# Reading expert weights from the slot that holds them, by register-addressed weight loads, instead of copying them between slots

## The chip, the cores and the metric

One core of one Trainium2 chip. The time is the device time of one execution of the whole kernel, in microseconds (us). Medians are given with the number of runs. A ratio is the mean time of one kernel's fast runs over the mean time of the other's fast runs of the same rounds on the same chip, so it isn't quite the ratio of the medians that stand beside it.

The medians are over all executions; the ratios leave the slow ones out. The kernel before was run again in each group of runs; its medians there were 215.28, 216.62, 215.74 and 217.13 us. The last of these groups (the run with one register-addressed block, and shared_late) was on another chip than the other experiments.

## The reference

Eight sequences of 576 tokens. Each goes through linear attention (8 heads of 64), then as a whole through one of eight experts, chosen by the mean of its tokens:

```python
# attention (Shen): softmax of q over the head dim, of k over the tokens
kv  = einsum('bhsd,bhse->bhde', k_s, v)
x   = einsum('bhsd,bhde->bhse', q_s, kv)        # -> x[8, 576, 512]
# sentence-level mixture of experts
logits = x.mean(axis=1) @ w_gate                # [8, 8]
e_idx  = argmax(logits, axis=1)                 # one expert per sequence
h   = maximum(x[b] @ w1[e], 0)                  # w1[e]: 512 x 1024
out = gate[b] * (h @ w2[e])                     # w2[e]: 1024 x 512
```

The inputs are one fixed draw, in which the experts come out as 2, 3, 3, 1, 3, 3, 4, 6. The kernel may not rely on that: it finds the expert of each sequence while it runs.

## The kernel before

TensorE computes in fp16, but for the gates' small matmuls (64 of the 1703 in the profile, f32). The weights of an expert lie in one of five slots of a ring in SBUF; sequence b has slot b mod 5. If an expert is already in the ring (a small history, searched on VectorE, says in which slot), its load from memory is skipped by a condition, and VectorE copies it from the source slot `src` into the sequence's own slot. If it was loaded fresh, `src` is the slot itself, and the same copies copy it onto itself. So there are always four copies per sequence, two of w1 and two of w2:

```python
    def fetch(b, w_all, part):
        if "src" not in seqs[b]:
            seqs[b]["src"] = nc.values_load(seqs[b]["sidx"][0:1, 0:1], engines=[ET.DVE], ...)
        ...
        copy = nc.vector.tensor_copy(
            out=w_all[:, b % NS, cs, fs],
            in_=w_all[:, ds(seqs[b]["src"], 1), cs, fs].rearrange("p o c f -> p (o c) f"),
        )

    def moe(b):
        xt = seqs[b]["xt"]
        w1_sb, w2_sb = w1_all[:, b % NS], w2_all[:, b % NS]      # constant addresses
        ...
        for fc in range(NF):                    # 8 column blocks of the first layer
            for c in range(ND):                 # 4 wide matmuls, 512 tokens
                nc.tensor.matmul(phm, lhsT=w1_sb[:, c, fsl], rhs=xt[:, c, 0:SM], ...)
            for c in range(ND):                 # 4 narrow ones, the other 64 tokens
                nc.tensor.matmul(pht[...], lhsT=w1_sb[:, c, fsl], rhs=xt[:, c, SM:S], ...)
            ...
            yield                               # attention of later sequences is woven in here
```

One `matmul` becomes two instructions on TensorE, a weight load and a matmul (the profile counts 1703 of each). The first layer of a sequence is 8 blocks of 8 such pairs.

The softmax here doesn't subtract the row's maximum and nothing guards it: scores larger than these inputs give would overflow.

Of the kernel before, what the change touches and what calls it, by code (L numbers as in the profile page):

```python
# [9 lines left out]
FP32 = mybir.dt.float32  # L10
# [3 lines left out]
ALU = mybir.AluOpType  # L14
AX = mybir.AxisListType
ET = mybir.EngineType
# [3 lines left out]
def kernel(  # L20
# [15 lines left out]
    nc = tc.nc  # L36

    B, H, S, Dh = q.shape
    D, E = moe_w_gate.shape
    F = moe_w1.shape[2]  # L40
    J = S // 64
    SM = 512
# [35 lines left out]
    ones_row = consts.tile([1, 128], FP16)  # L78
    nc.vector.memset(ones_row, 1.0)
    hist = consts.tile([1, 8], FP32)  # L80
    nc.vector.memset(hist, -1.0)
    held = consts.tile([1, 8], FP16)
    own = consts.tile([1, NS, 8], FP32)
    nc.vector.memset(own, 0.0)
# [23 lines left out]

    out_p = out.rearrange("b (p j) d -> b p j d", j=J)

    ins, halves, seqs, issued, copies = {}, {}, {}, {}, {}

    def load(n, names="qkv"):
        if n >= 2 * B:
# [146 lines left out]
    def gate_step(b):  # L261
        pooled = seqs[b]["pooled"] if b else seqs["pooled"]
        pg = bank("x") if b else seqs["qb"][0][:, 32:64]
        for c in range(ND):
            nc.tensor.matmul(
                pg[0:1, 0:E], lhsT=pooled[:, c:c + 1], rhs=wg_sb[:, c, :],
                start=(c == 0), stop=(c == ND - 1),
            )
        zz = gat_pool.tile([1, E], FP32, name="zz")
        nc.vector.tensor_single_scalar(out=zz, in_=pg[0:1, 0:E], scalar=1.0 / S, op=ALU.mult)  # L270
        mx8 = gat_pool.tile([1, 8], FP32, name="mx8")
        nc.vector.max(out=mx8, in_=zz)
        eidx = gat_pool.tile([1, 8], U32, name="eidx")
        nc.vector.max_index(out=eidx, in_max=mx8, in_values=zz)
        slot = b % NS
        sidx = None
        if b:
            same = gat_pool.tile([1, 8], FP32, name="same")
            nc.vector.tensor_tensor(
                out=same, in0=hist, in1=eidx[0:1, 0:1].to_broadcast([1, 8]), op=ALU.is_equal  # L280
            )
            score = gat_pool.tile([1, 8], FP32, name="score")
            nc.vector.scalar_tensor_tensor(
                out=score, in0=same, scalar=2.0, in1=own[:, slot], op0=ALU.mult, op1=ALU.max
            )
            top = gat_pool.tile([1, 8], FP32, name="top")
            nc.vector.max(out=top, in_=score)
            fresh = gat_pool.tile([1, 1], U32, name="fresh")
            nc.vector.tensor_single_scalar(out=fresh, in_=top[:, 0:1], scalar=1.0, op=ALU.is_equal)
            sidx = gat_pool.tile([1, 8], U32, name="sidx")  # L290
            nc.vector.max_index(out=sidx, in_max=top, in_values=score)
        nc.vector.tensor_copy(out=hist[:, slot:slot + 1], in_=eidx[0:1, 0:1])

        gone = (b + 2) % NS
        nc.vector.memset(hist[:, gone:gone + 1], -1.0)
        nmx = gat_pool.tile([1, 1], FP32, name="nmx")
        nc.vector.tensor_single_scalar(out=nmx, in_=mx8[:, 0:1], scalar=-1.0, op=ALU.mult)
        e_val = nc.values_load(
            eidx[0:1, 0:1], engines=[ET.Pool], min_val=0, max_val=E - 1,
            skip_runtime_bounds_check_because=IN_RANGE,  # L300
        )
        kw = {}
        if b:
            f_val = nc.values_load(
                fresh, engines=[ET.Pool], min_val=0, max_val=1,
                skip_runtime_bounds_check_because="is_equal gives 0 or 1",
            )
            kw = dict(cond=(f_val == 1))
        w1_src = moe_w1[ds(e_val, 1)].rearrange("o (h c e) f -> h e (o c) f", h=2, c=ND)
        nh = 1 if b else 2  # L310
        issued[b] = []
        for fh in range(nh):
            fs = slice(fh * F // nh, (fh + 1) * F // nh)
            for h in range(2):
                issued[b].append(nc.gpsimd.dma_start(  # L315
                    out=w1_all[64 * h:64 * h + 64, slot, :, fs], in_=w1_src[h][:, :, fs], **kw
                ))
        seqs[b].update(zz=zz, nmx=nmx, sidx=sidx, e_val=e_val, kw=kw)
        if b:
            load_w2(b)  # L320
        for load_inst in issued[b]:
            for copy in copies.get(b - 1, ()):
                apart(load_inst, copy)

    def apart(first, second):
        tc.declare_no_dep(
            first.ins, second.ins,
            reason="the slot that b + 1 loads into is taken out of the history before b looks for its source",
        )
# [41 lines left out]
        nc.vector.tensor_tensor(out=gate, in0=gate, in1=pb[:, 0:1], op=ALU.add)  # L371
        seqs[b]["gate"] = gate

    def fetch(b, w_all, part):

        if "src" not in seqs[b]:
            seqs[b]["src"] = nc.values_load(
                seqs[b]["sidx"][0:1, 0:1], engines=[ET.DVE], min_val=0, max_val=NS - 1,
                skip_runtime_bounds_check_because=IN_RANGE,
            )  # L380
        if w_all is w1_all:
            cs, fs = slice(0, ND), slice(part * (F // 2), (part + 1) * (F // 2))
        else:
            cs, fs = slice(part * (NF // 2), (part + 1) * (NF // 2)), slice(0, D)
        copy = nc.vector.tensor_copy(  # L385
            out=w_all[:, b % NS, cs, fs],
            in_=w_all[:, ds(seqs[b]["src"], 1), cs, fs].rearrange("p o c f -> p (o c) f"),
        )
        copies.setdefault(b, []).append(copy)
        for load_inst in issued.get(b + 1, ()):  # L390
            apart(copy, load_inst)

    def moe(b):
        xt = seqs[b]["xt"]
        w1_sb, w2_sb = w1_all[:, b % NS], w2_all[:, b % NS]
        hsb = h_pool.tile([128, NF, S], FP16, name="hsb")
        pht = bank("ht")
        for fc in range(NF):
            phm = bank("mm")
            fsl = slice(fc * 128, (fc + 1) * 128)  # L400
            for c in range(ND):
                nc.tensor.matmul(  # L402
                    phm, lhsT=w1_sb[:, c, fsl], rhs=xt[:, c, 0:SM],
                    start=(c == 0), stop=(c == ND - 1),
                )
            for c in range(ND):
                nc.tensor.matmul(  # L407
                    pht[:, fc * ST:(fc + 1) * ST], lhsT=w1_sb[:, c, fsl], rhs=xt[:, c, SM:S],
                    start=(fc == 0 and c == 0), stop=(fc == NF - 1 and c == ND - 1),
                )  # L410
            nc.scalar.activation(out=hsb[:, fc, 0:SM], in_=phm, func=AF.Relu)  # L411
            if fc == NF - 1:
                nc.scalar.activation(
                    out=hsb[:, :, SM:S], in_=pht.rearrange("p (c s) -> p c s", c=NF), func=AF.Relu
                )
            yield
        gate = seqs[b]["gate"]
        for st in range(4):
            po = bank("mm")
            for fc in range(NF):  # L420
                nc.tensor.matmul(  # L421
                    po, lhsT=hsb[:, fc, st * 128:st * 128 + 128], rhs=w2_sb[:, fc, :],
                    start=(fc == 0), stop=(fc == NF - 1),
                )
                if fc == 3:
                    yield
            osb = o_pool.tile([128, D], FP32, name="osb")
            nc.scalar.mul(osb, po, gate)  # L428
            for jj in range(2):
                nc.sync.dma_start(out=out_p[b, :, 2 * st + jj], in_=osb[64 * jj:64 * jj + 64])  # L430
            yield
        po = bank("mm")
        HD = D // 2
        for fc in range(NF):
            for dh in range(2):
                nc.tensor.matmul(  # L436
                    po[64 * dh:64 * dh + 64, 0:HD], lhsT=hsb[:, fc, SM:S],
                    rhs=w2_sb[:, fc, dh * HD:(dh + 1) * HD], start=(fc == 0), stop=(fc == NF - 1),
                )
        osb = o_pool.tile([128, HD], FP32, name="osb_t")  # L440
        nc.scalar.mul(osb, po[:, 0:HD], gate)
        for dh in range(2):
            nc.sync.dma_start(
                out=out_p[b, :, J - 1, dh * HD:(dh + 1) * HD], in_=osb[64 * dh:64 * dh + 64]
            )
        yield
# [8 lines left out]
    def at(t, fn, *args):  # L455
        ticks.setdefault(t, []).append((fn, args))
# [10 lines left out]
    at_gate(2, 1)  # L467
    at(9.5, load, 5)
    at(9.6, load, 6)
    places = [(15, 25), (30, 35), (41, 46), (58, 64), (74, 80), (91, 97)]  # L470
    for b in range(2, B):
        for i in range(2):
            n, t = 2 * b + i, places[b - 2][i]
# [8 lines left out]
            at(t - 4.25, scale_q, n, nc.gpsimd)  # L482
        at_gate(places[b - 2][1] + 5.5, b)
    for b in range(1, B):
        for part in range(2):
            at(NU * b - 1 + 0.5 * part, fetch, b, w1_all, part)
            at(NU * b + 4 + part, fetch, b, w2_all, part)
    times = sorted(ticks)
    done = [0]

# [89 lines left out]
```

## Time and profile before

| | before |
|---|---|
| time, median of 3 | 215.05 us (213.42 to 219.71) |
| span of the profiled execution, granted TensorE clock | 213.7 us, 0.919 |
| TensorE busy | 176.0 us, 82% of the span |
| VectorE busy, of which copies between slots | 119.0 us, 29.5 us |
| seven first layers (sequences 1 to 7), from the first wide matmul of each to the first matmul of its second layer | 74.55 us |
| idle TensorE in front of them, waiting for copies | 12.78 us |

The last two rows are read from TensorE's timeline and add up the single stretches. The group of the narrow matmuls is one of the page's costliest groups (the page is the summary of the profile; the numbers are the count, then busy us and mean ns, then idle time just before them):

```profile
L407 PE MATMUL ht<-xt,w_all 128*128 128x64 f16 x256 | 18.6, 197 | 0.0
```

All 256 narrow matmuls together kept TensorE busy for 18.6 us and never waited: they hide behind the wide ones (in sequence 7's layer four of them are busy for 0.28 us, and the next wide one starts 0.11 us after the first of them).

### The profile page before, as it was taken

How to read it: one execution, taken by the hardware profiler on the slowest of the kernel's cores; microseconds unless marked ns; L12 is line 12 of the kernel's file. 1: busy time of each engine (PE TensorE's matmuls, PEld its weight loads, DVE VectorE, ACT ScalarE, POOL GpSimd, SP SyncE). 2: the span in 40 equal slices, each digit the busy share in tenths (PEclk: the TensorE clock that was granted, in tenths of full speed). 3: DMA queues.
4: the chain of work that ended last, by engine and by line, in shares of the span. 5: the costliest groups of instructions: out<-in, count | busy, mean ns of one | idle time of the engine just before them, and what ended most of it. 6: DMA issues, size and time to landing. Idle time of an engine off the chain costs nothing.

```text
span 213.7 us, 4597 instructions
## 1 busy us (share of the span) xinstructions
PE 176.0 (82%) x1703; PEld 94.3 (44%) x1703; DVE 119.0 (56%) x365; ACT 113.3 (53%) x177; POOL 62.2 (29%) x70
## 2 busy tenths in 40 slices
PE   6357499996999379797498999999777979999990
PEld 6344345443545135433244454535343535545540
DVE  0757935137697977994455757974755365222000
ACT  2776854672974418651266728653582334546541
POOL 2143600630266330373026230730084302300000
PEclk9965559999999859999969999999996999999999
DMA  6999899999998998999999595814379751999044
GB/s 187 379 390 369 123 206 298 230 217 297 398 389 253 395 348 276 336 323 240 275 244 324 158 328 119 300 36 114 76 110 200 141 123 48 160 186 270 1 113 110
DMA packets 28582, 48.55 MB, mean 227 GB/s; under 512 B 2960, under 2 KB 10128, under 8 KB 28560
## 3 DMA queue, kind: packets, MB, share of 16 engines
q1 hardware_dynamic: 19472, 37.76, 53.5%
q0 software_dynamic: 8544, 10.49, 30.1%
q8 instruction: 13, 0.21, 0.4%
q10 hardware_dynamic: 544, 0.02, 0.1%
q14 instruction: 9, 0.07, 0.1%
HBM read 61.88 MB, written 9.44 MB: 334 GB/s over the span
## 4 chain that ended last, share of the span: by engine, by line
PE 43%; DMA 25%; DVE 19%; issue 5%; POOL 3%; ACT 1%; DVEq 1%; POOLq 0%; ACTq 0%
PE mm L421 19%; DMA w_all<-in_moe_w_dram 17%; PE mm L402 15%; DVE w_all L385 7%; DMA v_in<-in_v_dram 5%; DVE qs L142 4%; DMA wg_sb<-in_moe_w_gate_dram 3%; PE kv L160 2%; PE mm L436 2%; PE x L219 2%; PE ht L407 2%; DVE kv L170 2%; DVE qt L189 2%; DVE xt L230 1%; PE kv L181 1%
## 5 line engine op out<-in xcount | busy, mean ns | idle before, releaser
L402 PE MATMUL mm<-xt,w_all 128*128 128x512 f16 x256 | 69.9, 405 | 12.8 <-DVE w_all L385 12.8
L411 ACT ACTIVATE hsb<-mm 128x512 f16<-128x512 f32 x64 | 37.8, 596 | 45.0 <-PE mm L402 44.5
L421 PE MATMUL mm<-w_all,hsb 128*128 128x512 f16 x256 | 60.6, 383 | 0.4 <-DMA w_all<-in_moe_w_dram 0.3
L428 ACT ACTIVATE osb<-mm,gate 128x512 f32<-128x512 f32 x32 | 22.0, 687 | 37.3 <-PE mm L421 31.0
L385 DVE COPY w_all<-w_all 128x2048 f16 x28 | 29.5, 1052 | 14.0 <-DMA w_all<-in_moe_w_dram 13.7
L402 PEld LDWEIGHTS <-w_all 128*128 128x128 f16 x256 | 21.4, 102 | 34.8 <-DVE w_all L385 14.5
L145 POOL TENSOR_TENSOR eq<-eq,qsi 128x1152 f16<-128x1152 f16 x13 | 28.0, 2152 | 26.6 <-DVE qsi L144 25.5
L421 PEld LDWEIGHTS <-hsb 128*128 128x128 f16 x256 | 23.3, 98 | 26.2 <-issue 0.8
L230 DVE CUSTOM_DVE_ANT_0 xt<-x,ones_f 128x576 f16<-128x576 f32 x26 | 19.3, 743 | 17.1 <-PE x L220 17.1
L315 POOL DMA_DIRECT2D w_all<-in_moe_w_dram x18 | 8.2, 455 | 66.1 <-DMA w_all<-in_moe_w_dram 24.8
L142 DVE TENSOR_REDUCE qs<-eq 128x18 f32<-128x1152 f16 x16 | 21.5, 1343 | 10.1 <-ACT eq L124 10.1
L132 POOL CAST va<-v_in 128x1152 f16<-128x1152 f32 x14 | 17.7, 1261 | 24.7 <-DMA v_in<-in_v_dram 24.6
L407 PEld LDWEIGHTS <-w_all 128*128 128x128 f16 x256 | 17.0, 101 | 17.1 <-issue 3.3
L124 ACT ACTIVATE eq<-q_in 128x1152 f16<-128x1152 f32 x16 | 18.5, 1159 | 2.3 <-DMA q_in<-in_q_dram 2.3
L136 ACT ACTIVATE ek<-k_in 128x1152 f16<-128x1152 f32 x16 | 18.6, 1161 | 1.1 <-DMA k_in<-in_k_dram 1.1
L407 PE MATMUL ht<-xt,w_all 128*128 128x64 f16 x256 | 18.6, 197 | 0.0
L219 PE MATMUL x<-qt,kv 128*128 128x512 f16 x32 | 14.0, 438 | 2.7 <-DVE kv L170 0.8
L168 DVE RECIPROCAL icv<-kv 128x1 f32<-128x1 f32 x30 | 4.8, 162 | 18.7 <-PE kv L181 18.2
L160 PE MATMUL kv<-va,ek 64*128 64x129 f16 x270 | 11.7, 230 | 3.3 <-POOL va L132 2.1
L160 PEld LDWEIGHTS <-ek 64*128 64x128 f16 x288 | 10.1, 102 | 8.2 <-issue 6.6
L181 PE MATMUL kv<-ident,eq 64*128 64x64 f16 x270 | 7.3, 196 | 7.6 <-POOL eq L145 3.0
L170 DVE SCALAR_TENSOR_TENSOR kv<-kv,icv,blkmask 128x128 f16<-128x128 f32 x30 | 10.5, 351 | 1.1
(80 smaller groups left out, 133.8 us busy)
## 6 DMA issues: line engine op xcount, KB each, us to landing
w_all<-in_moe_w_dram POOLq DMA_DIRECT2D x30, 512.0 KB
q_in<-in_q_dram SPq DMA_DIRECT2D x16, 576.0 KB, 6.6
k_in<-in_k_dram SPq DMA_DIRECT2D x16, 576.0 KB, 9.2
v_in<-in_v_dram SPq DMA_DIRECT2D x16, 576.0 KB, 9.1
out_dram<-osb SPq DMA_DIRECT2D x64, 128.0 KB, 5.5
w_all<-in_moe_w_dram POOLq DMA_DIRECT2D x4, 256.0 KB
out_dram<-osb_t SPq DMA_DIRECT2D x16, 64.0 KB, 2.2
wg_sb<-in_moe_w_gate_dram ACTq DMA_DIRECT2D x2, 8.0 KB, 5.3
```

Of the source, the lines that this page charges most:

```text
L124: nc.scalar.activation(out=eq.rearrange("p j n d -> p n j d"), in_=ins.pop((n, "q")), func=AF.Exp)
L136: nc.scalar.activation(out=ek.rearrange("p j n d -> p n j d"), in_=ins.pop((n, "k")), func=AF.Exp)
L142: nc.vector.tensor_reduce(out=qs, in_=eq, op=ALU.add, axis=AX.X)
L145: eng.tensor_tensor(out=eq, in0=eq, in1=qsi.unsqueeze(3).to_broadcast([128, J, 2, Dh]), op=ALU.mult,)
L160: nc.tensor.matmul(kps[g][:, 0:129], lhsT=ek[r, j], rhs=va[r, j], start=(j == 0), stop=(j == J - 1),)
L230: nc.vector.tensor_tensor_reduce(out=xt[:, c, :], in0=px[:, 0:S], in1=ones_f32.to_broadcast([128, S]), scale=1.0, scalar=0.0, op0=ALU.mult ...
L385: copy = nc.vector.tensor_copy(out=w_all[:, b % NS, cs, fs], in_=w_all[:, ds(seqs[b]["src"], 1), cs, fs].rearrange("p o c f -> p (o c) f"),)
L402: nc.tensor.matmul(phm, lhsT=w1_sb[:, c, fsl], rhs=xt[:, c, 0:SM], start=(c == 0), stop=(c == ND - 1),)
L407: nc.tensor.matmul(pht[:, fc * ST:(fc + 1) * ST], lhsT=w1_sb[:, c, fsl], rhs=xt[:, c, SM:S], start=(fc == 0 and c == 0), stop=(fc == NF - ...
L411: nc.scalar.activation(out=hsb[:, fc, 0:SM], in_=phm, func=AF.Relu)
L421: nc.tensor.matmul(po, lhsT=hsb[:, fc, st * 128:st * 128 + 128], rhs=w2_sb[:, fc, :], start=(fc == 0), stop=(fc == NF - 1),)
L428: nc.scalar.mul(osb, po, gate)
```

## The change

PE (TensorE) reads w1 straight from slot `src`: the address of each weight load and of the matmul behind it is worked out from a register that holds `src`. This is done by register instructions, which the profile shows as records of TensorE's sequencer, marked PEldq: one for each of these weight loads and matmuls, 896 in all. How far these records are ahead of the array's is called the lead; in the kernel before it was 0.97 us at sequence 7 (191.87 to 192.84). The two copies of w1 per sequence go; those of w2 stay. Since a reused w1 is no longer copied on, only slots that were really loaded may serve as sources, so the history changes too. The core of the diff:

```diff
+    def find(b):
+        seqs[b]["src"] = nc.values_load(seqs[b]["sidx"][0:1, 0:1], engines=[ET.PE], ...)
+
+    def w1_of(b, c, cols):
+        if b == 0:
+            return w1_all[:, 0, c, cols]
+        return w1_all[:, ds(seqs[b]["src"], 1), c, cols].rearrange("p o f -> p (o f)")
...
-                nc.tensor.matmul(
-                    phm, lhsT=w1_sb[:, c, fsl], rhs=xt[:, c, 0:SM],
+                use(b, nc.tensor.matmul(
+                    phm, lhsT=w1_of(b, c, fsl), rhs=xt[:, c, 0:SM],
...            (the narrow matmuls likewise; fetch() keeps only w2)
-        nc.vector.tensor_copy(out=hist[:, slot:slot + 1], in_=eidx[0:1, 0:1])
+        if b:                                   # remember the expert only if it was loaded
+            nc.vector.tensor_single_scalar(out=loaded, in_=top[:, 0:1], scalar=1.0, op=ALU.is_equal)
+            nc.vector.scalar_tensor_tensor(out=hist[:, slot:slot + 1], in0=eidx[0:1, 0:1],
+                scalar=1.0, in1=loaded, op0=ALU.add, op1=ALU.mult)
...
-    places = [(15, 25), (30, 35), (41, 46), (58, 64), (74, 80), (91, 97)]
+    places = [(15, 25), (31, 36), (42, 47), (58, 64), (74, 80), (91, 97)]
```

More of the change, by code (lines that the diff above doesn't have):

```diff
@@ L80 @@
     hist = consts.tile([1, 8], FP32)
-    nc.vector.memset(hist, -1.0)
+    nc.vector.memset(hist, 0.0)
     held = consts.tile([1, 8], FP16)
@@ L109 @@
     out_p = out.rearrange("b (p j) d -> b p j d", j=J)
-    ins, halves, seqs, issued, copies = {}, {}, {}, {}, {}
+    ins, halves, seqs, issued, uses = {}, {}, {}, {}, {}
     def load(n, names="qkv"):
@@ L278, in gate_step @@
             same = gat_pool.tile([1, 8], FP32, name="same")
-            nc.vector.tensor_tensor(
-                out=same, in0=hist, in1=eidx[0:1, 0:1].to_broadcast([1, 8]), op=ALU.is_equal
+            nc.vector.scalar_tensor_tensor(
+                out=same, in0=hist, scalar=-1.0, in1=eidx[0:1, 0:1].to_broadcast([1, 8]),
+                op0=ALU.add, op1=ALU.is_equal,
             )
@@ L291, in gate_step @@
             nc.vector.max_index(out=sidx, in_max=top, in_values=score)
-        nc.vector.tensor_copy(out=hist[:, slot:slot + 1], in_=eidx[0:1, 0:1])
+        if b:
+            loaded = gat_pool.tile([1, 1], FP32, name="loaded")
+            nc.vector.tensor_single_scalar(out=loaded, in_=top[:, 0:1], scalar=1.0, op=ALU.is_equal)
+            nc.vector.scalar_tensor_tensor(
+                out=hist[:, slot:slot + 1], in0=eidx[0:1, 0:1], scalar=1.0, in1=loaded,
+                op0=ALU.add, op1=ALU.mult,
+            )
+        else:
+            nc.vector.tensor_single_scalar(
+                out=hist[:, slot:slot + 1], in_=eidx[0:1, 0:1], scalar=1.0, op=ALU.add
+            )
         gone = (b + 2) % NS
-        nc.vector.memset(hist[:, gone:gone + 1], -1.0)
+        nc.vector.memset(hist[:, gone:gone + 1], 0.0)
         nmx = gat_pool.tile([1, 1], FP32, name="nmx")
@@ L321, in gate_step @@
         for load_inst in issued[b]:
-            for copy in copies.get(b - 1, ()):
-                apart(load_inst, copy)
+            for op in uses.get(b - 1, ()):
+                apart(load_inst, op)
     def apart(first, second):
@@ L372, in gate_spread, with fetch @@
         seqs[b]["gate"] = gate
-    def fetch(b, w_all, part):
-        if "src" not in seqs[b]:
-            seqs[b]["src"] = nc.values_load(
+    def find(b):
+        seqs[b]["src"] = nc.values_load(
+            seqs[b]["sidx"][0:1, 0:1], engines=[ET.PE], min_val=0, max_val=NS - 1,
+            skip_runtime_bounds_check_because=IN_RANGE,
+        )
+    def w1_of(b, c, cols):
+        if b == 0:
+            return w1_all[:, 0, c, cols]
+        return w1_all[:, ds(seqs[b]["src"], 1), c, cols].rearrange("p o f -> p (o f)")
+    def fetch(b, part):
+        if "dsrc" not in seqs[b]:
+            seqs[b]["dsrc"] = nc.values_load(
                 seqs[b]["sidx"][0:1, 0:1], engines=[ET.DVE], min_val=0, max_val=NS - 1,
@@ L380, in fetch, with use @@
             )
-        if w_all is w1_all:
-            cs, fs = slice(0, ND), slice(part * (F // 2), (part + 1) * (F // 2))
-        else:
-            cs, fs = slice(part * (NF // 2), (part + 1) * (NF // 2)), slice(0, D)
-        copy = nc.vector.tensor_copy(
-            out=w_all[:, b % NS, cs, fs],
-            in_=w_all[:, ds(seqs[b]["src"], 1), cs, fs].rearrange("p o c f -> p (o c) f"),
-        )
-        copies.setdefault(b, []).append(copy)
+        cs = slice(part * (NF // 2), (part + 1) * (NF // 2))
+        use(b, nc.vector.tensor_copy(
+            out=w2_all[:, b % NS, cs],
+            in_=w2_all[:, ds(seqs[b]["dsrc"], 1), cs].rearrange("p o c f -> p (o c) f"),
+        ))
+    def use(b, op):
+        uses.setdefault(b, []).append(op)
         for load_inst in issued.get(b + 1, ()):
-            apart(copy, load_inst)
+            apart(op, load_inst)
     def moe(b):
         xt = seqs[b]["xt"]
-        w1_sb, w2_sb = w1_all[:, b % NS], w2_all[:, b % NS]
+        w2_sb = w2_all[:, b % NS]
         hsb = h_pool.tile([128, NF, S], FP16, name="hsb")
@@ L401, in moe @@
             for c in range(ND):
-                nc.tensor.matmul(
-                    phm, lhsT=w1_sb[:, c, fsl], rhs=xt[:, c, 0:SM],
+                use(b, nc.tensor.matmul(
+                    phm, lhsT=w1_of(b, c, fsl), rhs=xt[:, c, 0:SM],
                     start=(c == 0), stop=(c == ND - 1),
-                )
+                ))
             for c in range(ND):
-                nc.tensor.matmul(
-                    pht[:, fc * ST:(fc + 1) * ST], lhsT=w1_sb[:, c, fsl], rhs=xt[:, c, SM:S],
+                use(b, nc.tensor.matmul(
+                    pht[:, fc * ST:(fc + 1) * ST], lhsT=w1_of(b, c, fsl), rhs=xt[:, c, SM:S],
                     start=(fc == 0 and c == 0), stop=(fc == NF - 1 and c == ND - 1),
-                )
+                ))
             nc.scalar.activation(out=hsb[:, fc, 0:SM], in_=phm, func=AF.Relu)
@@ L484 @@
     for b in range(1, B):
+        at(NU * b - 3, find, b)
         for part in range(2):
-            at(NU * b - 1 + 0.5 * part, fetch, b, w1_all, part)
-            at(NU * b + 4 + part, fetch, b, w2_all, part)
+            at(NU * b + 4 + part, fetch, b, part)
     times = sorted(ticks)
```

## The prediction

> **What bounds the kernel now.** I read the page's chain first, then the costliest groups, then TensorE's timeline at the seven places where one expert's block ends and the next begins.
>
> ```profile
> PE 43%; DMA 25%; DVE 19%; issue 5%; POOL 3%; ACT 1%; DVEq 1%; POOLq 0%; ACTq 0%
> ...
> L402 PE MATMUL mm<-xt,w_all 128*128 128x512 f16 x256 | 69.9, 405 | 12.8 <-DVE w_all L385 12.8
> L385 DVE COPY w_all<-w_all 128x2048 f16 x28 | 29.5, 1052 | 14.0 <-DMA w_all<-in_moe_w_dram 13.7
> ```
>
> TensorE carries the chain, and its only large idle time inside the expert part is in front of the first layer (L402): 12.8 us, all charged to VectorE's copies of the weights between slots. The timeline shows the single gaps (start, duration, then the idle time in front):
>
> ```profile
> 51.03 1.04 PE L402 MATMUL mm<-xt,w_all 128*128 128x512 f16 x4 [1.84 <-DVE w_all L385]
> ...
> 75.96 1.89 PE L402 MATMUL mm<-xt,w_all 128*128 128x512 f16 x4 [4.79 <-DVE w_all L385]
> ...
> 105.89 1.04 PE L402 MATMUL mm<-xt,w_all 128*128 128x512 f16 x4 [2.74 <-DVE w_all L385]
> ...
> 191.85 1.06 PE L436 MATMUL mm<-w_all,hsb 128*64 128x256 f16 x16
> 192.84 1.04 PE L402 MATMUL mm<-xt,w_all 128*128 128x512 f16 x4
> 193.72 0.28 PE L407 MATMUL ht<-xt,w_all 128*128 128x64 f16 x4
> ```
>
> The other gaps are 0.47, 1.47, 1.47 and 0 us (sequences 4, 5, 6, 7). The last lines are a first layer with nothing in its way: one column block (4 wide, 4 narrow matmuls) follows the other after 0.98 us, so 8 blocks take 7.85 us. The sequencers' records give the rest:
>
> ```profile
> L385 DVEq FUSED_REGOPS  x28: 65/67/75, 49.9 to 196.2; - x28
> ...
> L402 PEldq EVENT_SEMAPHORE  x9: 51/51/51, 28.3 to 191.9; - x9
> ```
>
> The first is what a register-held address costs today: one instruction of 65 to 75 ns on VectorE's sequencer before each copy. The second tells how far TensorE's sequencer runs ahead: for the last sequence it reached the wait in front of the first layer at 191.87, when the 16 pairs of L436 were just starting. In every undisturbed case it was 14 pairs (28 instructions, about 1 us) ahead.
>
> [...] the 65 to 75 ns are sequencer time while VectorE computes. [...] The trace shows 28 instructions of lead, and I use 28. [...] The trace has three halvings in the expert part, at 73.3, 107.4 and 162.0, each after a window in which TensorE was 30 to 45% busy; windows with 1.5 us idle (over half busy) kept the full clock. [...] the copy at 73.28 took 2.62 us beside a GpSimd multiply, the lone ones 0.69.
>
> **The change part by part.**
>
> Removed: 14 of 28 copies (w1), some 13 us of VectorE time, and TensorE's wait for them. What comes back, gap by gap. Sequence 1: the load had landed only at 50.2, so 0.75 of 1.84. Sequence 2: nearly all of 4.79, plus about 2.1 us of half clock that the gap caused, plus 1 to 1.5 us at 87 us where TensorE waited for a sum that stood behind a 2.3 us copy. Sequence 3: the load landed at 105.08, so 0.8 of 2.74. Then 0.47, 1.47, 1.47. Sum 0.75 + 4.8 + 2.1 + 1.2 + 0.8 + 0.5 + 1.5 + 1.5 = 13.2 us. If nothing else changed, the time would be 202.
>
> Added on TensorE: the built order shows one fused register instruction in front of every weight load and every matmul of the first layer of sequences 1 to 7: 7 x 64 x 2 = 896, of which 868 do four operations (multiply, add, multiply, add). They aren't engine work, so they only matter if the sequencer falls behind. Its cost per slot (register instruction plus the instruction it serves), from two engines:
> - VectorE: 75 ns for four operations, 50 ns to the next sequencer instruction, 18 ns more when a copy stands between: 143 ns[...].
> - GpSimd[...]: 50 to 56 ns, then 31 ns; with 14.5 ns for pushing one TensorE instruction (18 static transposes after an empty queue went at 29 ns per pair): 96 to 101.
> I take 106 ns, an estimate. A column block has 16 slots: 1.70 us of sequencer against 0.98 us of array. A whole first layer: 64 x 0.212 = 13.6 us against 7.85. The other instructions in it (projection, transposes, 4 to 80 of them) add up to 1.2 us at 14.5 ns each. Against that stand about 1.1 us of lead, which sequences 1 and 3 don't have, since their sequencer blocks at the load's semaphore.
>
> First layer of each sequence, before -> after, and the running shift of its end (after minus before), gap included:
> - 1: 8.3 -> 13.7; start 0.75 earlier: +4.6.
> - 2: 13.9 (with half clock and waits) -> 13.7; gap 4.8 gone: -0.4. Its end releases the next gate, which before ran one block earlier in it: the gate comes 1 us later.
> - 3: bound by its load, 16.6 us after that gate before, so the start is +0.2; 12.0 -> 14.8: +3.0.
> - 4: gap -0.5; 10.1 -> 13.7: +6.1.
> - 5: gap -1.5; 13.0 (with 2.5 us of waits for GpSimd that the slower pace hides) -> 13.7: +5.3.
> - 6: gap -1.5; 8.4 -> 12.7: +8.1.
> - 7: 7.85 -> 12.6: +12.8.
>
> Moved: history. Only a slot that was loaded counts as a source now. From the reference's fixed draw the experts are 2, 3, 3, 1, 3, 3, 4, 6. Before, sequence 5 finds expert 3 in the copy that sequence 2 made; afterwards only sequence 1's load counts, which has left the ring by then, so sequence 5 is loaded: six loads for five, 4 MB more from HBM. It is issued around 133, when the queues are at 58 to 76% busy, and sequence 4 gives it over 16 us, so I expect the data in time; [...] 0.6 to 0.75 us for each of four instead of 0.04, just before a cast and a multiply that TensorE waits for: +0.5 us. The shift of two projection steps by one tick lets the gate of sequence 2 go first; it is what makes its new register load on TensorE (about 0.3 us, as on VectorE) cheap. The new history arithmetic is one or two tiny instructions of 0.14 us per gate, off the path.
>
> Sum: +13 us by this table, 228. I pull it a little towards the low side of the slot, 224 to 225, because the two engines that I scale from disagree: each 10 ns of slot moves the end by 7 to 8 us (1.28 us per layer, six layers that count), so 97 ns would give 221 and 85 ns about the time of before.
>
> **Rivals.**
> (a) The register work is hidden and the gaps come back: 202 to 209. For it: register instructions run beside the array, and in this trace TensorE's sequencer is always ahead. Against: the lead is 28 instructions, one microsecond, and the deficit is 5 us per layer; a slot would have to cost under 70 ns.
> (b) It balances: slot 80 to 90 ns, losses eat the gains, 211 to 219. For it: GpSimd's shortest figures. Against: TensorE's own semaphore instruction takes 51 ns where ScalarE's takes 17, so its sequencer is no quick one.
> (c) The half-fed array lets the clock halve: a block has 0.98 us of work in 1.70 us, 57% busy, just above what kept the full clock in this trace. At half clock a block is 1.95 us, so it would add up to 0.25 us x 8 per layer: 235 to 240.
> (d) The extra load for sequence 5 becomes the wait: up to 3 us more if its first half lands after 155.
>
> **Range and chances.** The slot's error is about 9 ns either way, 7 us; (a) and (b) widen the low side, (c) the high one: 211 to 240. Faster needs a slot under some 82 ns, or stalls vanishing that I have left in: 0.12. Within 2%: 0.18. Slower: 0.70.
>
> **What would show it.** Right: in first layers of sequences 4 to 7 TensorE's narrow matmuls (L407 before) come singly, 0.2 us apart, without a named releaser, and a block takes 1.5 to 1.9 us; the gap in front of the first layers of 2, 4, 5 and 6 is under 0.5 us; second layers keep 0.22 us per wide matmul; the register instructions on TensorE's sequencer show 50 to 60 ns. Wrong: blocks of 1.0 us (the slot is hidden), or a copy, a load or GpSimd named in front of the first layers again. Then the gain of up to 13 us stands, and the time is under 209.

What the trace shows: in the 3.40 us before each of the three halvings TensorE was busy for 1.26, 1.51 and 0.97 us; and GpSimd's DMA instruction took 0.6 to 0.75 us for each of the four parts of an expert that was loaded, and 0.04 us for each part of one that was skipped, which is the difference that the +0.5 us is made of. The 106 ns, between GpSimd's 96 to 101 and VectorE's 143, stand as the author's estimate alone. The 14.5 ns in them are an estimate too: in the trace 29 ns is the step of two transposes, each a weight load and a matmul. The table came to +13 us, 228 us in all, and the prediction was 224 to 225 us.

## The result, and the profile after

The changed kernel is correct and takes **231.92 us** (median of 4, 230.74 to 232.19) against 215.28 of before on the same chip: ratio **1.079**, 95% interval 1.071 to 1.088. It is slower by 8%. The span went from 213.7 to 230.1 us, and the granted clock rose from 0.919 to 0.946.

The page of the changed kernel: the shares of the chain that ended last, and three of the costliest groups.

```profile
PE 67%; DMA 19%; issue 5%; DVE 4%; POOL 1%; POOLq 0%; ACTq 0%; ACT 0%; DVEq 0%
...
L426 PE MATMUL mm<-xt,w_all 128*128 128x512 f16 x256 | 70.1, 387 | 3.4 <-DMA w_all<-in_moe_w_dram 1.8
...
L431 PE MATMUL ht<-xt,w_all 128*128 128x64 f16 x256 | 40.8, 192 | 5.7 <-issue 0.2
...
L406 DVE COPY w_all<-w_all 128x2048 f16 x14 | 19.9, 1421 | 8.6 <-DMA w_all<-in_moe_w_dram 6.8
```

Read it against before. The wait for VectorE in front of the wide matmuls is gone (12.8 us, now one wait of 1.8 us for a load), and VectorE's share of the chain fell from 19 to 4%. So the change did what it was for. But the narrow matmuls went from 18.6 to 40.8 us of busy time although each takes the same 0.19 us: they no longer overlap, and they have 5.7 us of idle time in front of them that no releaser explains ("issue" is time in which the engine waited for nothing that the profile shows). TensorE's share rose from 43 to 67%. The timeline of sequence 7's first layer, where nothing else is going on, shows it block by block (start, duration, what):

```profile
202.99 1.04 PE L426 MATMUL mm<-xt,w_all 128*128 128x512 f16 x4
203.86 0.31 PE L431 MATMUL ht<-xt,w_all 128*128 128x64 f16 x4
204.21 1.06 PE L426 MATMUL mm<-xt,w_all 128*128 128x512 f16 x4
205.12 0.90 PE L431 MATMUL ht<-xt,w_all 128*128 128x64 f16 x4
206.05 1.06 PE L426 MATMUL mm<-xt,w_all 128*128 128x512 f16 x4
```

The first block still goes at nearly the old pace (1.22 us, and its narrow matmuls take 0.31 us). Then the pace is 1.84 us and more: from the second block at 204.21 to the end of the layer at 217.15 there are seven blocks, 1.85 us each, against 0.98 before. The windows over the whole layer (length; busy time of TensorE, its weight loads, VectorE, ScalarE, GpSimd; granted clock; DMA), before and then after:

```profile
192.84:200.69 7.85, 7.85 (x66) 4.07 (x65) 1.39 (x2) 4.65 (x8) 0.00 (x0) 1.00 0.59 169
```

```profile
203.00:217.15 14.15, 12.65 (x66) 5.90 (x65) 0.00 (x0) 5.21 (x9) 0.00 (x0) 1.00 0.16 37
```

The same 66 matmuls, at full clock, with VectorE and GpSimd idle, take 14.15 instead of 7.85 us. The records of the sequencer at line L426 point to what keeps them apart (minimum, median and maximum ns, first and last start):

```profile
L426 PEldq FUSED_REGOPS  x448: 46/55/60, 48.2 to 216.1; - x150
```

There are 448 fused register instructions at this line and 448 at the narrow one. One takes 55 ns. In the trace the next one starts 113 ns (median) after the one before, so the instruction that it serves costs another 58 ns. In sequence 7's layer the 128 of them start from 202.01 to 217.02, 118 ns apart on average, since a few slots take 133 to 270 (a slot of the sequencer, as the prediction uses the word, is a register instruction and the instruction that it serves; it has nothing to do with the slots of the ring). The first starts 0.98 us ahead of the first matmul: that is the lead, and it pays for the first block only. In this lead the array is still at the second layer of sequence 6, with constant addresses, and the register instructions already come 109 to 119 ns apart (after one step of 240 with a semaphore in it). So the spacing isn't made by the array.

Where the span's 16.4 us come from, added up over sequences 1 to 7 from both timelines:

| | before | after | difference |
|---|---|---|---|
| start of sequence 1's first layer, its wait left out | 49.19 | 49.13 | -0.06 |
| seven first layers | 74.55 | 103.32 | +28.77 |
| waits in front of them | 12.78 | 1.80 | -10.98 |
| the rest (second layers, woven-in attention) | 72.23 | 70.96 | -1.27 |

### The profile page after: what moved, and what is told of

It reads as the page before. It is cut to its first block, busy times and chain, and to the rows that moved or that the text cites. A ratio compares the mean times of both kernels' runs of the same rounds, so it can differ in the third digit from the quotient of the medians.

```text
span 230.1 us, 5480 instructions
## 1 busy us (share of the span) xinstructions
PE 203.0 (88%) x1703; PEld 105.5 (46%) x1703; DVE 111.6 (48%) x358; ACT 115.5 (50%) x177; POOL 64.6 (28%) x70
## 4 chain that ended last, share of the span: by engine, by line
PE 67%; DMA 19%; issue 5%; DVE 4%; POOL 1%; POOLq 0%; ACTq 0%; ACT 0%; DVEq 0%
PE mm L426 25%; PE mm L445 18%; PE ht L431 13%; DMA w_all<-in_moe_w_dram 12%; DMA v_in<-in_v_dram 5%; PE mm L460 3%; PE kv L160 3%; DMA wg_sb<-in_moe_w_gate_dram 3%; PE x L219 2%; PE kv L181 1%; DVE qs L142 1%; PE x L265 1%; DVE qt L189 1%; DVE kv L170 1%; POOL w_all L327 1%
## 5 line engine op out<-in xcount | busy, mean ns | idle before, releaser
L426 PE MATMUL mm<-xt,w_all 128*128 128x512 f16 x256 | 70.1, 387 | 3.4 <-DMA w_all<-in_moe_w_dram 1.8
L435 ACT ACTIVATE hsb<-mm 128x512 f16<-128x512 f32 x64 | 38.3, 598 | 58.2 <-PE mm L426 57.9
L431 PE MATMUL ht<-xt,w_all 128*128 128x64 f16 x256 | 40.8, 192 | 5.7 <-issue 0.2
L426 PEld LDWEIGHTS <-w_all 128*128 (+1 forms) x256 | 23.4, 98 | 32.3 <-issue 8.8
L431 PEld LDWEIGHTS <-w_all 128*128 (+1 forms) x256 | 22.7, 97 | 30.6 <-issue 5.3
L327 POOL DMA_DIRECT2D w_all<-in_moe_w_dram x18 | 9.6, 537 | 63.5 <-DVE nmx L309 28.5
L406 DVE COPY w_all<-w_all 128x2048 f16 x14 | 19.9, 1421 | 8.6 <-DMA w_all<-in_moe_w_dram 6.8
L132 POOL CAST va<-v_in 128x1152 f16<-128x1152 f32 x14 | 16.8, 1197 | 25.2 <-DMA v_in<-in_v_dram 25.0
```

Source lines behind the costliest of these rows:

```text
L406: use(b, nc.vector.tensor_copy(out=w2_all[:, b % NS, cs], in_=w2_all[:, ds(seqs[b]["dsrc"], 1), cs].rearrange("p o c f -> p (o c) f"),))
L426: use(b, nc.tensor.matmul(phm, lhsT=w1_of(b, c, fsl), rhs=xt[:, c, 0:SM], start=(c == 0), stop=(c == ND - 1),))
L431: use(b, nc.tensor.matmul(pht[:, fc * ST:(fc + 1) * ST], lhsT=w1_of(b, c, fsl), rhs=xt[:, c, SM:S], start=(fc == 0 and c == 0), stop=(fc = ...
L435: nc.scalar.activation(out=hsb[:, fc, 0:SM], in_=phm, func=AF.Relu)
```

## The experiments

The theory: TensorE's sequencer, at 113 ns or more for each pair of register instruction and served instruction, is what sets the pace of the first layers. The rivals: reading from another slot costs by itself; the lost copies or the extra load for sequence 5 do; a fixed cost per sequence; a cost of register-addressed weight loads in the array. "First layers" below is the sum of the seven stretches, as in the table above.

### The changed kernel without registers

```diff
+    KNOWN = [0, 1, 1, 3, 1, 0, 1, 2]            # the slots that this draw finds
-        return w1_all[:, ds(seqs[b]["src"], 1), c, cols].rearrange("p o f -> p (o f)")
+        return w1_all[:, KNOWN[b], c, cols]
```

(It gives the right result for this draw only; it is a measuring device, not a kernel.)

> The changed kernel with each sequence's source slot written in as a constant (the slots that this draw finds: 0, 1, 1, 3, 1, 0, 1, 2), so that TensorE has no register instruction and no register load; copies of w1 gone, history and loads as in the changed kernel. Theory (TensorE's sequencer at 113 ns a slot makes the first layers of sequences 1 to 7 long): a column block is back at about 0.98 us, the first layers at about 8 us each, and the time is 202 to 207 us. Rival (the lost copies, the slots read from, or the extra load for sequence 5 cost the time themselves): still over 220 us.

Measured: 209.92 us (median of 4; before 216.62), ratio 0.974 (0.961 to 0.987); first layers 75.98 us. The page's groups:

```profile
L426 PE MATMUL mm<-xt,w_all 128*128 128x512 f16 x256 | 66.8, 392 | 3.3 <-DMA w_all<-in_moe_w_dram 3.3
...
L431 PE MATMUL ht<-xt,w_all 128*128 128x64 f16 x256 | 18.2, 195 | 0.0
```

The narrow matmuls are back at 18.2 us, and 22 us of time have gone with the register instructions (and their seven register loads) alone. Copies, slots and loads are those of the changed kernel, so none of them costs the time. The theory holds. But the size was a miss: I expected 202 to 207, since 13 us of copy waits were to come back. Only 6 to 7 us did. The timeline shows new waits in the middle of the kernel:

```profile
82.88 0.35 PE L265 MATMUL x<-wg_sb,pooled 128*1 128x8 f32 x8 [2.24 <-DVE pooled L230]
...
99.27 1.87 PE L426 MATMUL mm<-xt,w_all 128*128 128x512 f16 x4 [3.26 <-DMA w_all<-in_moe_w_dram]
...
113.58 0.16 PE L380 MATMUL x<-hl,ones_row 1*128 1x2 f16 x1 [2.15 <-DVE hl L372]
...
134.19 0.43 PE L181 MATMUL kv<-ident,eq 64*128 64x64 f16 x18 [2.13 <-POOL eq L145]
```

The waits in front of the first layers fell from 12.78 to 3.26 us, but the layers grew by 1.4 us and the rest of sequences 1 to 7 by 0.9, because TensorE, now earlier at these points, waits there for the gate of the next sequence, its load and GpSimd. The array's clock belongs to this. From sequence 1's first layer to the last matmul it ran at half speed for 13.65 us before (three times) and again for 13.65 us here (from 84.5, 98.2 and 135.7 us, each within 2 us of one of these waits), so what was to come back from half clock did not. In the changed kernel it was 3.41 us. (Another 1.0 us was lost before sequence 1, in a wait for w2 of sequence 0: 2.44 us here, 0.28 before.)

### The kernel before with registers

```diff
+    slots = consts.tile([1, NS], U32)           # 0, 1, 2, 3, 4
+    def w1_of(b, c, cols):
+        if b == 0:
+            return w1_all[:, 0, c, cols]
+        return w1_all[:, ds(seqs[b]["own"], 1), c, cols]...    # "own" is b % NS, from slots
-                    phm, lhsT=w1_sb[:, c, fsl], rhs=xt[:, c, 0:SM],
+                    phm, lhsT=w1_of(b, c, fsl), rhs=xt[:, c, 0:SM],
```

> The kernel before, with all its copies and its history, but with TensorE reading its own slot (the same addresses as before) through a register: only the 896 register instructions are added. Theory: about 1.81 us a column block, 29 us more in seven first layers less what the waits for copies hide, so 238 to 246 us. Rival (register work is harmless, reading another slot or the extra load is what costs): within 2% of before, 211 to 220 us.

Measured: 252.13 us (median of 4), ratio 1.168 (1.154 to 1.181); first layers 108.21 us. The wide and narrow matmuls and the copies:

```profile
L423 PE MATMUL mm<-xt,w_all 128*128 128x512 f16 x256 | 72.5, 399 | 18.2 <-DVE w_all L406 16.3
...
L428 PE MATMUL ht<-xt,w_all 128*128 128x64 f16 x256 | 41.4, 193 | 6.3 <-issue 0.4
```

Same addresses, same copies, same loads as before, and 36 us more. The verdict for the registers is clear; the expected range was 6 us too low. Two reasons are in the numbers. The waits for copies did not get hidden: they grew from 12.8 to 16.3 us. In sequences 1, 5 and 6 they are 0.8 us longer each (1.84, 1.47 and 1.47 us became 2.64, 2.29 and 2.28), a little more than one copy of 0.69 us. The traces show why: before, the first matmul of sequence 1 starts at 51.03, right after the first copy (ended 50.98) and beside the second; here it starts at 54.97, after the second (ended 54.83). And the first layers are 4.9 us longer than in the changed kernel, mainly because the lead is lost. In sequences 1 to 6 the sequencer stops between its first two register instructions for 1.5 to 7.4 us, and the first matmul follows right after. In the changed kernel only sequence 3, which waits for its load, has such a stop; the other five had a lead of 0.97 to 1.22 us each there. Their layers grew by 0.7, 2.1, 1.1, 0.7 and 0.7 us (in sequence 2 half clock until 91.7 us is part of it). A stretch of 3.1 us was also lost before sequence 1, in the wait for w2 of sequence 0 and at a lower clock.

### Half of the instructions, spread out

`matmul()` works the address out twice, for the weight load and for the matmul that names the weights again (in the changed kernel's trace, 448 register instructions for the 224 register-addressed matmuls of each line). Here the load alone takes the register address; the matmul names a constant stand-in, whose own weight load is taken out of the program:

```diff
+                if b:
+                    lhs = ident                  # a stand-in; what counts is what was loaded
+                    use(b, nc.tensor.ldweights(w1_of(b, c, fsl), tile_position=(0, 0)))
-                use(b, nc.tensor.matmul(phm, lhsT=w1_of(b, c, fsl), ...))
+                nc.tensor.matmul(phm, lhsT=lhs, ...)
...
+    # after the build: drop the load of ident behind each register-addressed load
```

> The changed kernel, but only the weight load takes its address from the register; the matmul behind it names a stand-in and uses what was loaded, so its own register instruction is gone: 448 instead of 896. Weight loads still read the found slot. Theory: a block costs the sequencer 8 x (113 + 14.5) = 1.02 us against 0.98 us of array, so it is nearly hidden: 203 to 209 us. Rival (what costs is the weight load from a register address itself, not the instructions in front of both): a block stays near 1.8 us, over 225 us; a time about halfway, 217, would say that the lead counts for nothing.

Measured: 210.32 us (median of 4), ratio 0.978 (0.966 to 0.990), correct; first layers 75.43 us. That is a little above the 203 to 209 us expected, which did not count the new waits. Its register instructions at the wide loads, and sequence 7's first layer:

```profile
L429 PEldq FUSED_REGOPS  x224: 51/55/60, 48.6 to 195.0; - x112
```

```profile
187.69 1.04 PE L430 MATMUL mm<-xt,ident 128*128 128x512 f16 x4
188.56 0.28 PE L439 MATMUL ht<-xt,ident 128*128 128x64 f16 x4
188.68 1.03 PE L430 MATMUL mm<-xt,ident 128*128 128x512 f16 x4
189.54 0.28 PE L439 MATMUL ht<-xt,ident 128*128 128x64 f16 x4
189.66 1.03 PE L430 MATMUL mm<-xt,ident 128*128 128x512 f16 x4
```

The instruction is as long as ever (55 ns), and every weight load still takes its address from the register, but a block is back at 0.98 to 0.99 us. From one register instruction to the next it is now 133 ns: 113 for the register instruction and its load, 20 for what is plain behind it. Eight times 133 is 1.06 us a block, a hair over what the array needs, and the lead pays the difference: the layer took 7.98 us against 7.85. So a register-addressed load didn't stall the array here; it was the sequencer's time that counted.

### A quarter of the instructions

The same, with one weight load for the wide and the narrow matmul of the same rows: 224 register instructions in all.

```diff
             for c in range(ND):
                 if b: use(b, nc.tensor.ldweights(w1_of(b, c, fsl), tile_position=(0, 0)))
                 nc.tensor.matmul(phm, lhsT=lhs, rhs=xt[:, c, 0:SM], ...)
-            for c in range(ND):
                 nc.tensor.matmul(pht[...], lhsT=lhs, rhs=xt[:, c, SM:S], ...)
```

> As loads_by_register, and one weight load serves the wide and the narrow matmul of the same 128 rows: 224 register instructions, 32 weight loads a first layer instead of 64, and matmuls in the order wide, narrow, wide, narrow. Theory: 4 x 113 + 8 x 14.5 = 0.57 us of sequencer a block against 0.96 to 0.98 us of array, wholly hidden: the time of known_slots within 1%, so 201 to 207 us, faster than before by some 5%. Rival (the register-addressed load stalls the array by itself): 32 stalls a layer are left, over 215 us.

Measured: 210.75 us (median of 4), ratio 0.977 (0.967 to 0.987), correct; first layers 76.68 us, sequence 7's exactly 7.85. The time is that of the kernel without registers, as the theory asked, so the 32 loads that are left per layer cost nothing; the 201 to 207 us were off by the same new waits. Two plain matmuls now stand behind each register-addressed load, and from one register instruction to the next it is still 133 ns (median): so the 20 ns are not a price of each plain matmul. And one weight load served two matmuls: 224 loads for 448 matmuls, with a right result.

### A dose of registers: one block, four blocks

```diff
-        if b == 0:
-            return w1_all[:, 0, c, cols]
+        if b == 0 or cols.start >= 4 * 128:      # and 1 * 128 in the other run
+            return w1_all[:, KNOWN[b], c, cols]
```

> The changed kernel with register addressing in the first four of the eight column blocks only; the last four use the known slots as constants. A dose between known_slots (none, ratio 0.974) and the changed kernel (all, 1.079). Theory (each register-addressed block after the first microsecond of lead costs 1.81 instead of 0.98 us): 4 x 0.83 = 3.3 us a layer less about 1 us of lead where there is some, so 2.3 to 3.3 us in each of seven layers, part of it over waits that are there anyway: known_slots plus 9 to 17 us, 219 to 227 us. Rival (a fixed cost per sequence, such as the register load of the slot number or a fill of the queue): all of the 22 us, about 232, as soon as one block uses the register.

> The changed kernel with register addressing in the first of eight column blocks only. Theory (TensorE's sequencer runs about 1 us ahead and can lose 0.83 us in one block without leaving the array empty): first layers of sequences 6 and 7 at 8.4 to 8.7 and 7.9 to 8.1 us as in known_slots, and its ratio, 0.974 plus or minus 0.006. Rival (each block costs its 0.83 us at once): first layers 9.2 and 8.7 us, ratio 0.98 to 1.00.

Measured: with four blocks 216.15 us (median of 5), ratio 1.001 (0.995 to 1.007), first layers 84.62 us; with one block 211.83 us (median of 4), ratio 0.975 (0.963 to 0.986), sequences 6 and 7 at 8.43 and 7.89 us. Sequence 7 with four blocks:

```profile
192.65 1.04 PE L428 MATMUL mm<-xt,w_all 128*128 128x512 f16 x4
...
193.89 1.15 PE L428 MATMUL mm<-xt,w_all 128*128 128x512 f16 x4
...
195.79 1.10 PE L428 MATMUL mm<-xt,w_all 128*128 128x512 f16 x4
...
197.65 1.10 PE L428 MATMUL mm<-xt,w_all 128*128 128x512 f16 x4
...
199.31 1.02 PE L428 MATMUL mm<-xt,w_all 128*128 128x512 f16 x4
...
200.29 1.03 PE L428 MATMUL mm<-xt,w_all 128*128 128x512 f16 x4
```

Blocks of 1.24, 1.90, 1.86 and 1.66 us, and then at once 0.98: the pace follows the registers block by block. One block alone costs 0.04 us in sequence 7 and nothing in sequence 6: it is paid by the lead. That is what a bound sequencer with about a microsecond in hand does, and what a cost per block or per sequence does not.

The four-block run also fell below its expected range (219 to 227). Where the array does nothing but the layer, the cost is as expected: 2.4, 2.4 and 2.7 us for sequences 1, 6 and 7. For sequences 2 to 5 it is +1.4, -1.1, +0.8 and 0.0 us: in the kernel without registers those layers contain the waits quoted above, and slower blocks fill waits before they cost anything. Compare this run with half of the instructions spread out: both have 64 register instructions a layer, 216.15 against 210.32 us. What counts is how far the sequencer falls behind, not how many register instructions there are.

### Three operations instead of four

VectorE multiplies the slot number by the slot's size once per sequence, so the fused instruction does one operation less; the 896 instructions stay.

```diff
+            nc.vector.tensor_single_scalar(out=soff, in_=sidx[0:1, 0:1], scalar=float(ND * F), op=ALU.mult)
-        return w1_all[:, ds(seqs[b]["src"], 1), c, cols].rearrange("p o f -> p (o f)")
+        return w1_flat[:, ds(seqs[b]["src"] + (c * F + cols.start), 128)]
```

> The changed kernel, but VectorE multiplies the slot number by the slot's size once per sequence, so the fused register instruction in front of each weight load and matmul does three operations instead of four; their number stays at 896. Theory (sequencer time per slot is what counts, and part of it goes per operation): a slot falls from 113 to 103 to 109 ns, and at 7 to 8 us of time for each 10 ns the kernel takes 3 to 7 us less than the changed one, 225 to 229 us. Rival (the cost is per instruction, whatever is fused into it): the slot stays at 113 ns and the time at 231 to 233 us.

Measured: 224.60 us (median of 4), ratio 1.042 (1.036 to 1.049); first layers 95.54 us.

```profile
L431 PEldq FUSED_REGOPS  x448: 37/46/51, 48.7 to 208.1; - x150
```

46 instead of 55 ns, and in the trace 104 instead of 113 from one to the next. 9 ns times 128 slots times seven layers are 8.1 us; the first layers shrank by 7.8 and the time by 7.3 (across two groups of runs). This is the exchange rate between the sequencer's nanoseconds and the kernel's microseconds, measured. (The time came in just under the expected 225 to 229: the slot was as expected, and each nanosecond was worth a little more than the 0.7 to 0.8 us I had used.)

### The extra load alone

```diff
-    nc.vector.memset(hist, -1.0)
+    nc.vector.memset(hist, 0.0)
...          (the changed kernel's history in the kernel before; all copies and constant addresses stay)
```

> The kernel before with the changed kernel's history alone: sequence 5 is loaded again (4 MB more), all 28 copies and constant addresses stay. The prediction gave this part +0.5 us. Theory: 0 to +2 us over before, ratio 1.00 to 1.01. Rival (the extra load delays what follows, and so explains why known_slots gained only some 6 us where 13 were expected): +4 to +7 us, ratio 1.02 to 1.03.

Measured: 217.22 us (median of 6; before 215.74), ratio 1.0046 (0.9989 to 1.0103). About 1 us, not told apart from nothing. It explains neither the loss nor the small gain without registers.

### What is left of the copies' gain

If the new waits in the middle are what ate the gain, removing their causes should bring it back. In the quarter-instruction kernel, VectorE's two copies of w2 for sequence 2 ran beside a GpSimd multiply, and the gate of sequence 3 waited for what stood behind them. First step: VectorE's sum for sequence 4 (which lets that multiply start) comes after the copies.

```diff
-            at(t - 4.25, scale_q, n, nc.gpsimd)
+            at(t - (2.9 if n == 8 else 4.25), scale_q, n, nc.gpsimd)
```

> The kernel shared with one step moved: VectorE's sum and reciprocal for sequence 4's first half comes after sequence 2's two copies of w2 instead of before them, so that GpSimd's multiply no longer runs beside these copies (3.03 us for the two in shared, 1.4 alone). The theory of why the copies' return was small is that waits downstream took it over: here gate 3 waited 2.24 us for VectorE, and sequence 3's load then came 3.35 us late. Expected: gate 3 2 to 3 us earlier, the wait for sequence 3's load 0 to 1.5 us, and the time 1 to 3 us below shared, a ratio to before of 0.962 to 0.974. Rival: another wait (GpSimd's multiply for sequence 4, now later) takes its place, ratio 0.974 to 0.98 as in shared.

Measured: 210.85 us (median of 6), ratio 0.973 (0.967 to 0.980), first layers 76.18 us. The copies, in VectorE's timeline of the quarter-instruction kernel and then of this one:

```profile
79.75 3.03 DVE L406 COPY w_all<-w_all 128x2048 f16 x2
```

```profile
78.21 1.42 DVE L406 COPY w_all<-w_all 128x2048 f16 x2
```

The collision is gone and gate 3 comes 1.6 us earlier (81.93 instead of 83.51; 2 to 3 were expected). But the next wait stays as it was:

```profile
98.79 0.38 PE L430 MATMUL mm<-xt,ident 128*128 128x512 f16 x1 [3.32 <-DMA w_all<-in_moe_w_dram]
```

The time is on the border of both expectations, and the theory's part about this wait (0 to 1.5 us) failed: the load came 1.1 us earlier, and so did TensorE. From its issue to its landing (85.3 to 98.7 us) the DMA engines were full: the DMA view from 82 to 100 us shows 90% or more in 37 of its 40 slices. Second step, on top of the first: two groups of input loads that nobody needs yet are issued later.

```diff
-                at(t - 4.35, load, n + 3)
+                at({8: 46, 9: 50}.get(n, t - 4.35), load, n + 3)
```

> The kernel shared_tuned with two groups of input loads (q, k and v of sequence 5's second half and of sequence 6's first half, 3.5 MB) issued some five to eight blocks later, so that they no longer share the DMA queues with the load of sequence 3's expert, which in shared_tuned landed 15.6 us after issue (median of its four transfers) at 90 to 100% busy DMA engines. Theory (with the register work hidden, the waits of 2 to 3 us in the middle, above all for this load, are what is left of the copies' gain): the wait in front of sequence 3's first layer falls from 3.3 us to 0 to 1.5 us and the time to 206 to 209 us, ratio 0.957 to 0.968. Rival (the load isn't slowed by these inputs, or a later wait takes over): ratio 0.970 to 0.98.

Measured: **208.11 us** (median of 6; before 217.13), ratio **0.963** (0.957 to 0.968), correct; first layers 77.43 us.

```profile
95.83 0.38 PE L430 MATMUL mm<-xt,ident 128*128 128x512 f16 x1 [0.38 <-DMA w_all<-in_moe_w_dram]
```

The wait for the load fell from 3.32 to 0.38 us, and the time is inside the range expected. Not all came back: the next wait, for VectorE's part of a gate at 110 us, is now 4.04 us, and the half clock is still 13.65 us. This kernel beats both: 4% faster than before, and 24 us below the changed kernel (across chips, so roughly). It makes no use of the draw for its addresses, but the two moved steps were chosen on this draw's trace.

## Why the prediction was right, and where its size was off

By its own steps:

- **The mechanism was right.** "They only matter if the sequencer falls behind" is what the runs show: no registers, 209.92; registers within the array's pace, 210.32; registers beyond it, 231.92 us. The signs it named all came: narrow matmuls singly (in the trace 226 ns apart, two slots) with no named releaser; blocks of 1.85 us; no gap left in front of the first layers of sequences 2, 4, 5 and 6; second layers at 0.22 us per wide matmul; register instructions of 55 ns.
- **The mis-sized term was "I take 106 ns".** It measured 113 at the median and 118 on average over sequence 7's layer. 12 ns times 128 slots is 1.5 us a layer: 14.20 and 14.16 us where the prediction has 12.7 and 12.6 for sequences 6 and 7. Over seven layers its 94.9 us were 103.3. Of the two figures that it was taken from, VectorE's 143 ns lay above the measured slot and GpSimd's 96 to 101 below it. GpSimd's register instruction, 50 to 56 ns, was close to the 55 measured; what it misled about is the served instruction. The prediction took 14.5 ns for pushing it, an estimate from transposes with constant addresses. But 113 less 55 leaves 58 ns for an instruction that has a register in its address, against 20 for one or two plain matmuls. Why it takes so long was not shown by a run.
- **"I pull it a little towards the low side" was wrong.** The table's own sum was 228; the pull cost 4 of the 7.9 us by which 224 missed. Two sources that disagree were a reason for a wider range, not for a lower centre.
- **The lead was right**: about 1.1 us predicted, 0.98 in sequence 7, and one block of registers is free. Sequence 3 had none, as predicted, but sequence 1 had 0.97 us, which the prediction denied.
- **The returned waits were larger than "Sum 0.75 + 4.8 + ..." let through to the end.** In the table's running shifts they amount to some 8.5 us (94.9 less about 73.5 for the first layers is 21.4, and its last shift is 12.8); the runs show 12.3. Sequence 1 started 1.9 us earlier, not 0.75. This error and the slot's have opposite signs, and so, by luck, the sum looked better than its terms: the running shift was predicted as +4.6, -0.4, +3.0, +6.1, +5.3, +8.1, +12.8 and measured as +4.0, -0.9, +2.8, +7.3, +6.6, +10.2, +16.5 us.
- **"If nothing else changed, the time would be 202" was wrong**, though it wasn't put to the test by the change itself. Without registers it is 210, since waits for the gate, the load and GpSimd take over in sequences 2 to 5, and the 2.1 us of half clock that the sum has as returned did not come back (13.65 us at half clock in both). In the changed kernel the slow first layers hide these waits, so they don't show.
- **Rivals.** (a) and (b) fell with the slot. (c), a half clock, did not come: the clock row shows full speed through the first layers from sequence 1 on, but for 3.41 us at half speed from 106.15 us, after the one wait for a load (1.80 us), and TensorE counts as busy for 12.65 of 14.15 us in sequence 7's layer, not for the 57% that the prediction made of its useful work. (d) did not come either: no wait for sequence 5's load, and +0.5% for the extra load alone.

## What to carry to other kernels

An address from a register was paid on TensorE's sequencer, per instruction that used it, and it showed because the 16 slots of a block, 113 ns or more each, made it 1.85 us long where the array needs 0.98. To check another kernel, compare instructions per block times the cost of a slot (here 113 ns with four fused operations, 104 with three, and some 20 ns more where one or two plain matmuls follow) with the array's time for the block, and count what the sequencer is ahead as a one-time credit. If the addressing is still wanted, halve it before giving it up: address the weight load alone and let the matmuls behind it, wide and narrow, use what was loaded (210.32 and 210.75 us here, against 231.92). And the waits taken away in one place were only an upper bound of the gain: about half of 13 us went to the next waits and their half clock, and came back in part when those waits were looked at one by one.
